# Second-stage rows interleaved by thirds over the partitions, the opening's writes in halves on SyncE, and some evictions behind the first unit's passes

## The chip, the core and the metric

The kernel runs on one core of a Trainium2 chip. Five engines work beside each other, each through its own queue in program order: TensorE (PE; its weight loads are shown as PEld), VectorE (DVE), ScalarE (ACT), GpSimd (POOL) and SyncE (SP). SyncE, ScalarE and GpSimd also issue DMA transfers. The metric is the device time of one execution in microseconds (us).

## What is computed

```python
def _attn_ref(x):                       # x: 8 x 3008 x 256, float32
    X = np.fft.fft(x, axis=1)
    X = np.fft.fft(X, axis=2)
    return X.real.astype(np.float32)

def _moe_ref(x, w_gate, w_val, w_out):  # 24064 x 256; 256 x 1536 twice; 1536 x 256
    g = x @ w_gate
    gelu = 0.5 * g * (1.0 + erf(g * inv_sqrt2))
    val = x @ w_val
    return (gelu * val @ w_out).astype(np.float32)
```

The second function takes the first one's result as 24064 tokens of 256.

## The kernel before

**Splitting.** The 3008 = 64 x 47 points of a batch's sequence are transformed in two stages. The transform over the 256 channels is folded into the weights: `x` is folded into even and odd channel sums (`fold_x`), and the gate and value weights are multiplied by cosine and sine tables once (`gen_w`), giving `WE`, `WOP` and `WOM`. Since the result is real, one half of the sequence gives the other by mirrored rows, called plus and minus.

**First stage.** `load_x` brings a batch in three parts of eight row blocks into `xins` (three buffers of 1 MB). `fold_x` writes `xf`. `a_step(b, k)` makes two products of 128 x 128 with 128 x 256 into one PSUM bank and copies them to `S1`; twelve such steps make the 24 blocks of 128 rows. For batch 0 the banks go round four names; for the others all use `ps_d`, which has one buffer, so each step waits for the copy of the step before it.

**Turning.** The second stage needs other rows side by side. `z_write` stores blocks of `S1` to a scratch `z` in device memory; `z_read` reads it back into `Ap`, 96 partitions of 32 groups x 256. Partition 4 j + r holds rows 32 r to 32 r + 31 of block j. In the opening, block thirds are written from ScalarE's queue and read into 32 neighbouring partitions each. In the other batches there are two writes of 12 blocks and two reads, each of all 96 partitions but of 16 groups: the first read brings groups 0 to 15, the second groups 16 to 31.

**Second stage.** `b_steps(b, eo, q)` makes eight groups' products of 96 x 128 with a table `TP`, `TQ`, `T0P` or `T0Q` (47 columns), for even (`eo` 0) or odd (`eo` 1) channels, and `evac` copies them to `Y`. Each copies the first 24 columns, then the rest. `q` goes over four sets of eight groups. `TW` and `n_step` make one special row for the values' odd part (`NQ`), which goes through device memory (`n_first` for batch 0).

**Tables.** `phase_g`, `phase_c` and `phase_t` make arguments, `reduce_phase` brings them into range, `sin_g`, `sin_c` and `sin_t` take the sine on ScalarE. `cols_t` makes the columns that number the 96 partitions; with `phase_c` it runs on GpSimd in the opening.

**Units.** After the opening a loop runs over 288 units `u`: batch `b`, three column chunks and 12 blocks of 128 of the 1536 inner width; `i` counts the 36 units of a batch. A unit makes layer 1 for its block: `val_even`, `gate_minus` of the unit before, `gate_plus`, `val_odd` of the unit before, with VectorE's and GpSimd's products behind, and eight products of the layer 2 of an earlier chunk (`l2_steps`). Between the passes of a unit stand the next batch's second-stage steps (`fills`): `plan` gives the unit in which each begins. For batches after the first the odd set `q` = 0 begins at i = 18 and q = 2 at i = 23; in the first batch q = 0 begins at i = 21. At the end of unit i stand `fold_x` of a later batch, `a_step` for the next batch (k = i, in batch 0 k = i - 3), a `z_write` after k = 5 and k = 11, and the two `z_read` at k = 12 and 13. At the beginning of units (0, 14, 19) a part of the batch after the next is loaded, in batch 0 at (8, 12, 17). Batches 6 and 7 load nothing. `extra` puts the remaining weight products into units of batch 0.

**Order.** Every engine keeps the program's order (`_InOrder`). All transfers but the opening's three writes and the load of `w_out` go through SyncE's queue: x, weights, z, the special row and 360 stores of results.

**Warming.** `warm` issues products on `ps_d` that nobody reads.

Of the kernel before, what the change touches and what calls it, by code (L numbers as in the profile page):

```python
# [37 lines left out]
def kernel(  # L38
# [73 lines left out]
    col_q = const_pool.tile([128, 1], FP32)  # L112
# [42 lines left out]
    def ps_d():  # L155
        return psum.tile([128, 512], FP32, tag="d", bufs=1, name="ps_d")
# [40 lines left out]
    iota(_sub(rowk, [[1, 33]], 0), [[1, 33]], 0, 0)  # L197
    iota(_sub(rowk, [[1, 31]], 33), [[1, 31]], 1, 0)
    pool.tensor_scalar(rowk, rowk, 1.0 / 64.0, None, op0=ALU.mult)
    pool.memset(NQ[:, :512], 0.0)  # L200
    iota(_sub(rowc, [[1, 128]], 0), [[1, 128]], 0, 0)
    iota(_sub(rowc, [[1, 128]], 128), [[1, 128]], 0, 0)
    pool.memset(_sub(rowc, [[1, 1]], 128), 128.0)
    for k in range(2):
        iota(_sub(rowt, [[1, 2 * N2]], k * 2 * N2), [[1, 2 * N2]], 0, 0)
        iota(_sub(rowt, [[1, MID]], 4 * N2 + k * NJ), [[1, MID]], 0, 0)
        iota(_sub(rowt, [[1, MID - 1]], 4 * N2 + k * NJ + MID), [[1, MID - 1]], 1, 0)
    pool.memset(_sub(rowt, [[NJ, 2]], 4 * N2 + NJ - 1), 0.0)

    wst = []  # L210

# [66 lines left out]
    def cols_t():  # L278
        R = 2 * NJ
        cp = lambda t: _sub(t, [[1, 1]], 0, 0, R)  # L280
        p, ge, jj, f4 = cp(col_p), cp(col_bot), cp(col_j), cp(col_q)
        for t, a, c in ((jj, 0.5, -0.25), (f4, 0.25, -0.375)):
            pool.tensor_scalar(t, p, a, c, op0=ALU.mult, op1=ALU.add)
            pool.tensor_scalar(t, t, MAGIC, None, op0=ALU.add)
            pool.tensor_scalar(t, t, MAGIC, None, op0=ALU.subtract)
        pool.tensor_scalar(ge, jj, -2.0, p, op0=ALU.mult, op1=ALU.add)
        pool.tensor_scalar(cp(col_top), ge, -1.0, 1.0, op0=ALU.mult, op1=ALU.add)
        pool.tensor_scalar(jj, jj, float(HJ), None, op0=ALU.mult)
        pool.tensor_scalar(jj, f4, -float(N2), jj, op0=ALU.mult, op1=ALU.add)
        pool.tensor_scalar(jj, jj, 1.0 / N2, None, op0=ALU.mult)  # L290
        wide = lambda n: _sub(col_bot, [[0, n]], 0, 0, R)
        for o, n, b0, b1 in [(0, 2 * N2, 0.25, 0.25), (2 * N2, 2 * N2, 0.0, 0.25),
                             (4 * N2, NJ, 0.25, 0.0), (4 * N2 + NJ, NJ, 0.0, 0.0)]:
            pool.tensor_scalar(
                _sub(quat, [[1, n]], o, 0, R), wide(n), b1, b0, op0=ALU.mult, op1=ALU.add)

    def phase_t():
        R = 2 * NJ
        W = 4 * N2 + 2 * NJ
# [20 lines left out]
    redc = []  # L320

    def phase_c(t):
        pool.tensor_scalar(col_c[t], col_p, 128.0 * t, 1.0 / C, op0=ALU.add, op1=ALU.mult)
        both = red2_tile()
        redc.append(both)
        for o, n, b0 in ((0, 129, 0.25), (129, 127, 0.5)):
            pool.tensor_scalar(
                both[:, o : o + n], rowc[:, o : o + n], col_c[t], b0, op0=ALU.mult, op1=ALU.add)

    def reduce_c():  # L330
        for both in redc:
# [30 lines left out]
                    WOM[:, i, fs], WOP[:, i, fs], col_m, None, op0=ALU.mult)  # L362

    def gen_wn():
        ps = ps_d()
        for fc in range(NFC):
            for t in range(NCH):
                pe.matmul(
                    ps[:, fc : fc + 1], wb[(fc // 4 * 512, 1)][:, t, fc % 4 * 128 : fc % 4 * 128 + 128],
                    CW[:, t, 1, 0:1], start=(t == 0), stop=(t == NCH - 1))  # L370
        vec.tensor_copy(WNb[:, :], ps[:, :NFC])
        vec.tensor_copy(WN[:, :], WNb[:, :])
# [50 lines left out]
    def a_step(b, k):  # L423

        xf = xf_bufs[b % 2]
        if "S1" not in st[b]:
            st[b]["S1"] = S1_tile()
        S1 = st[b]["S1"]
        ps = (ps_g, ps_v, ps_o, ps_v)[k % 4]() if b == 0 else ps_d()
        for i in range(2):  # L430
            jj = 2 * k + i
            st[b]["mm"] = (pe.matmul(
                ps[:, i * C : (i + 1) * C], G[:, jj, :], _sub(xf, [[1, C]], jj * C),
                start=True, stop=True))
        dst = _sub(S1, [[1, 2 * C]], 2 * k * C)
        if k % 2 == 0 and (b == 0 and k >= 8 or b == 1 and k < 8):
            return (vec.tensor_copy(dst, ps))
        return (act.activation(dst, ps, AF.Copy))
# [6 lines left out]
            z[0:1, 0, :], ap=[[C, 128], [128 * C, nj], [1, C]], offset=z[j0, 0:1, :].offset)  # L445
        eng.dma_start(out=dst, in_=_sub(S1, [[C, nj], [1, C]], j0 * C))

    def z_read(b, g0, ng, j0=0, nj=HJ):
        if "Ap" not in st[b]:
            st[b]["Ap"] = Ap_tile()  # L450
        z, Ap = st[b]["z"], st[b]["Ap"]
        src = ap_replace(
            z[0:1, 0, :], ap=[[NG * C, 4 * nj], [1, ng * C]], offset=z[j0, g0 : g0 + 1, :].offset)
        sync.dma_start(
            out=_sub(Ap, [[1, ng * C]], g0 * C, 4 * j0, 4 * nj), in_=src)

    def b_steps(b, eo, q):

# [25 lines left out]
                        ps[r, o : o + N2], w, t[:, s : s + N2], start=True, stop=True))  # L484
            return run

        def evac():
            ps = box["ps"]
            if Ys[b] is None:
                Ys[b] = Y_tile()  # L490
            Y = Ys[b]
            g0 = 8 * q

            def copy(o, i):
                if b or q % 2:
                    (act.activation(o, i, AF.Copy))
                else:
                    (vec.tensor_copy(o, i))

            copy(  # L500
                _sub(Y, [[32, MID], [1, 8]], eo * YW + g0),
                _sub(ps, [[1, MID], [N2, 8]], 0))
            n2 = N2 - MID
            f = 1 if q == 0 else 0
            copy(
                _sub(Y, [[32, n2], [1, 8 - f]], eo * YW + 32 * MID + g0 + f - 1),
                _sub(ps, [[1, n2], [N2, 8 - f]], MID + f * N2))
            if q == 0:
                copy(
                    _sub(Y, [[32, n2]], eo * YW + 32 * MID + 31), ps[:, MID:N2])  # L510
                copy(
                    _sub(Y, [[1, 1]], eo * YW + NCOL - 1), ps[:, 8 * N2 : 8 * N2 + 1])

        steps = [mm(gi, False) for gi in range(8)]
        if eo == 1 and b == 0:
            steps += [mm(gi, True) for gi in range(8)]
        return steps, evac


    units = []  # L520
# [138 lines left out]
        return steps  # L659


    def warm(n, w):
        ps = ps_d()
        k = w.ap[0][1]
        for _ in range(n):
            pe.matmul(ps, w, _sub(NQ, [[1, 512]], 0, 0, k), start=True, stop=True)

    for t in range(NCH):
        phase_c(t)
    cols_t()  # L670
    still = _sub(NQ, [[1, 128]], 0)
    for i in (1, 0):
        load_w(0, i)
    phase_g(0)
# [5 lines left out]
    for i in range(3):  # L680
        if i:
            fold_x(0, i, vec)
        for k in range(4 * i, 4 * i + 4):
            a_step(0, k)
        warm((5, 2, 4)[i], still)
        z_write(0, 8 * i, 8, act)
        if i == 0:
            sin_g(2)
        z_read(0, 0, NG, 8 * i, 8)
    for i in (1, 0):  # L690
        load_w(512, i)
    load_x(1, 0)
# [1 line left out]
    for i in (1, 0):  # L694
        load_w(1024, i)
    load_x(1, 2)
    reduce_c()
    sin_c()
    pt = phase_t()
    cast_w(0)  # L700
    for i in (1, 0):
        gen_w(0, i, (ps_g, ps_v))
    warm(6, still)
    warm(6, _sub(st[0]["Ap"], [[1, 128]], 0, 0, 64))
    sin_t(*pt)
    act.activation(col_f[:, :], col_p[:, :], AF.Gelu)
    for eo in range(2):
        for q in range(4):
            steps, evac = b_steps(0, eo, q)
            for s in steps:  # L710
                s()
            evac()
    n_first(0)
    cast_w(512)
    load_wo()
    extra = {2: lambda: gen_w(512, 1, (ps_o, ps_o)), 3: lambda: gen_w(512, 0, (ps_o, ps_o)),
# [15 lines left out]
    for u in range(NU + 2):  # L732
# [2 lines left out]
        tail = None  # L735
        if u < NU:
            open_unit(u)
            loads = (0, 14, 19) if b else (8, 12, 17)
            if i in loads and b + 2 < B:
                load_x(b + 2, loads.index(i))  # L740
            if b + 1 < B:
                for what in plan[min(b, 1)].get(i, ()):
                    if what == "n":
                        tail = lambda b=b: n_step(b + 1)
                        continue
                    eo, q, lo, hi = what
# [13 lines left out]
                if l2q:  # L760
                    l2q.pop(0)()

        if u < NU:
            val_even(u)
            fill()
        if 0 < u <= NU:
            gate_minus(u - 1)
            fill()
        if u < NU:
            gate_plus(u, fill)  # L770
            if banks[u]["kd"] == 0:
                plus(banks[u])
# [13 lines left out]
        if u < NU:  # L786
# [57 lines left out]
```

## Time and profile before

Three runs took 658.94, 660.66 and 660.88 us. The profiled execution:

| | |
|---|---|
| its own time | 660.34 us |
| span from first to last instruction | 658.6 us |
| PE busy | 632.5 us, 96% of the span |
| PEld busy | 415.5 us, 63% |
| DVE busy | 529.8 us, 80% |
| ACT busy | 459.3 us, 70% |
| POOL busy | 477.1 us, 72% |
| moved by DMA | 82.69 MB, mean 126 GB/s |
| mean granted TensorE clock | 0.992 |

A line of the page by slices has 40 digits, each the busy share of a slice of 16.5 us in tenths; PEclk is the granted clock in tenths. The chain of waits goes back from the last instruction to whatever released each one. In lists by time, a row has its start, its length, engine, source line, operation, target and source tiles and how many were merged; since a helper issues nearly everything, the source line is L25 for most rows, and rows are told apart by their tiles. SPq is the queue in which SyncE issues transfers: the length there is the issuing, not the transfer. A row of waits names who waited, for whom, the microseconds, how often and the longest.

The opening in a few rows: the x loads are issued from 0.74 us on, the first fold begins at 6.26, the first product at 8.88, the third write of batch 0's z is issued at 16.97, weight products run from 20.20 to 24.0, the second stage from 29.01 to 32.88, and the units begin there.

### The profile page before, as it was taken

What the parts mean: (1) busy time and instruction counts of PE and PEld (TensorE: products, weight loads), DVE (VectorE), ACT (ScalarE), POOL (GpSimd) and SP (SyncE); (2) the same over time, 40 slices, a digit from 0 to 9 for tenths busy, and PEclk for the clock granted to TensorE, in tenths of its full rate; (3) what the DMA queues carried; (4) which work ended last, traced back from release to release, by engine and by line L of the source; (5) the groups of instructions that cost most, each with busy time, mean ns of one, the idle gap of its engine ahead of it and who ended that gap; (6) DMA issues with size and microseconds to landing.
All of it is one profiled execution on the core that took longest, in us unless ns stands there. A gap on an engine that the chain in (4) does not pass through costs nothing.

```text
span 658.6 us, 14004 instructions
## 1 busy us (share of the span) xinstructions
PE 632.5 (96%) x4593; PEld 415.5 (63%) x4647; DVE 529.8 (80%) x860; ACT 459.3 (70%) x976; POOL 477.1 (72%) x777
## 2 busy tenths in 40 slices
PE   4698999999999999999999999999999999999997
PEld 2344666666666666666666666676666666666666
DVE  8567877797868988698777988689887987789981
ACT  8477677767678676776677676786767766666662
POOL 8294899977897598886897778975986544745450
PEclk9889999999999999999999999999999999999999
DMA  8993822456233832348224652328321452211123
GB/s 297 270 328 112 237 75 56 136 153 199 71 109 83 248 112 63 112 125 263 65 49 142 161 193 69 110 82 250 114 59 52 126 140 60 49 44 37 47 49 77
DMA packets 66089, 82.69 MB, mean 126 GB/s; under 512 B 8031, under 2 KB 58943, under 8 KB 62528
## 3 DMA queue, kind: packets, MB, share of 16 engines
q1 hardware_dynamic: 61344, 79.44, 41.7%
q0 software_dynamic: 1552, 0.79, 0.9%
q10 hardware_dynamic: 3120, 1.57, 0.8%
q8 instruction: 36, 0.59, 0.4%
q14 instruction: 37, 0.30, 0.2%
HBM read 45.13 MB, written 37.44 MB: 125 GB/s over the span
## 4 chain that ended last, share of the span: by engine, by line
PE 89%; DVE 6%; DMA 2%; ACT 1%; issue 1%; ACTq 0%; DVEq 0%
PE ps_o L25 38%; PE ps_g L25 26%; PE ps_v L25 20%; PE ps_d L25 6%; DVE h L25 2%; DVE xf L25 1%; DMA z<-S 1%; DMA Ap<-z 1%; ACT gl L25 1%; DVE ev L25 1%; DVE red L25 1%; DVE S L25 0%; DVE dv L25 0%; DVE WOM L25 0%; DVE sa L25 0%
## 5 line engine op out<-in xcount | busy, mean ns | idle before, releaser
L25 ACT ACTIVATE gl<-ps_g 128x512 bf16<-128x512 f32 (+1 forms) x576 | 309.4, 587 | 147.2 <-PE ps_g L25 104.7
L25 POOL TENSOR_TENSOR h<-gl,dv 128x512 bf16<-128x512 bf16 (+1 forms) x216 | 246.8, 1143 | 147.1 <-DVE dv L25 101.7
L25 DVE TENSOR_TENSOR h<-gl,ps_v 128x512 bf16<-128x512 bf16 (+2 forms) x360 | 237.4, 676 | 102.8 <-ACT gl L25 84.9
L25 PE MATMUL ps_o<-Wo_sb,h 128*128 128x256 bf16 (+2 forms) x2304 | 296.7, 273 | 0.0
L25 PEld LDWEIGHTS <-h 128*128 128x128 bf16 (+2 forms) x2304 | 227.0, 100 | 65.2 <-issue 1.8
L25 DVE SCALAR_TENSOR_TENSOR ev<-nq,WN,ps_v 128x512 f32<-128x512 bf16 (+1 forms) x216 | 157.5, 729 | 2.8 <-PE ps_v L25 2.8
L25 POOL TENSOR_TENSOR xf<-xin 128x127 bf16<-128x127 f32 (+1 forms) x312 | 141.7, 475 | 7.7 <-DMA xin<-in_x_dram 7.7
L25 DVE SCALAR_TENSOR_TENSOR dv<-ev,ps_v 128x512 f32<-128x512 f32 (+1 forms) x216 | 144.2, 667 | 0.0
L25 PE MATMUL ps_v<-Y,WE 128*128 128x512 bf16 (+1 forms) x287 | 108.4, 378 | 0.2 <-issue 0.2
L25 PE MATMUL ps_g<-Y,WOM 128*128 128x512 bf16 (+1 forms) x288 | 107.7, 374 | 0.1
L25 PE MATMUL ps_g<-Y,WOP 128*128 128x512 bf16 (+1 forms) x281 | 105.3, 375 | 2.0
L25 PE MATMUL ps_v<-Y,WOP 128*128 128x512 bf16 (+1 forms) x281 | 105.7, 376 | 0.4
L25 PE MATMUL ps_g<-Y,WE 128*128 128x512 bf16 (+1 forms) x250 | 93.7, 375 | 0.0
L25 PEld LDWEIGHTS <-WOP 128*128 128x128 bf16 x576 | 56.0, 97 | 47.1 <-issue 1.1
L25 ACT ACTIVATE osb<-ps_o 128x512 f32<-128x512 f32 (+2 forms) x112 | 58.3, 535 | 33.0 <-PE ps_o L25 29.8
L25 PEld LDWEIGHTS <-WE 128*128 128x128 bf16 x576 | 56.2, 98 | 25.3 <-issue 1.9
L25 PEld LDWEIGHTS <-Ap 96*128 96x128 bf16 (+3 forms) x574 | 43.6, 98 | 39.1 <-issue 11.2
L25 ACT ACTIVATE S<-ps_d 128x512 bf16<-128x512 f32 x80 | 48.3, 603 | 3.5 <-PE ps_d L25 3.5
L25 PEld LDWEIGHTS <-WOM 128*128 128x128 bf16 x360 | 35.0, 97 | 16.6 <-issue 0.8
L25 PEld LDWEIGHTS <-G 128*128 128x128 bf16 x192 | 19.0, 100 | 33.3 <-ACT G L25 6.3
L25 ACT ACTIVATE Y<-ps_d 128x192 bf16<-128x192 f32 (+4 forms) x142 | 37.3, 349 | 0.6 <-PE ps_d L25 0.6
L25 PE MATMUL ps_d<-xf,G 128*128 128x256 bf16 x168 | 32.0, 272 | 2.0 <-DVE S L25 1.5
(107 smaller groups left out, 284.7 us busy)
## 6 DMA issues: line engine op xcount, KB each, us to landing
out_dram<-osb SPq DMA_DIRECT2D x360, 64.0 KB
xin<-in_x_dram SPq DMA_DIRECT2D x16, 1024.0 KB
z<-S SPq DMA_DIRECT2D x14, 768.0 KB
Ap<-z SPq DMA_DIRECT2D x14, 768.0 KB
xin<-in_x_dram SPq DMA_DIRECT2D x8, 896.0 KB
ngr<-nrow SPq DMA_DIRECT2D x7, 388.0 KB
wst<-in_moe_w_val_dram SPq DMA_DIRECT2D x3, 512.0 KB
wst<-in_moe_w_gate_dram SPq DMA_DIRECT2D x3, 512.0 KB
```

The lines of the kernel that those rows point to most:

```text
L25: return lambda *a, **k: self._tc.keep_in_program_order(call(*a, **k))
```

## The change

- **Rows.** The turning of all batches goes by thirds: third t has blocks 8 t to 8 t + 7, all 32 groups, and goes to partitions t, t + 3, t + 6 and so on. The columns and tables are made for that numbering (`col_q` is three columns now). In the loop the three reads stand at k = 12, 13 and 14 (two at 12 and 13 before); the writes stay at k = 5 and 11 with 12 blocks each. In batch 0 the third x load moves from unit 17 to 18; in the others the loads stay at (0, 14, 19).
- **Opening's transfers.** The writes go through SyncE; the second and third in halves of four blocks. The first read is issued between the halves of the second write, the other two at the end.
- **Table work.** `cols_t` is first on GpSimd, and the constant parts of `quat` are clears. `phase_c` moves from GpSimd to ScalarE (with constant bias columns) and behind the first stage. `phase_t` comes before it, `sin_t` before the weight products. The clear of NQ is gone.
- **Warming** multiplies `G` by `G`, 5, 2 and 10 products in the opening's steps and 6 ahead of the second stage, instead of 5, 2, 4, 6 and 6.
- **Banks.** `gen_wn` uses `ps_o`; `a_step` of batch 1 uses `ps_o` in steps 1, 3, 5 and 7.
- **First unit.** The odd sets' copies are split: the first 24 columns behind their products, the rest behind the four passes of unit 0, which are written out in a new order.

```diff
-    pool.memset(NQ[:, :512], 0.0)
-    iota(_sub(rowc, [[1, 128]], 0), [[1, 128]], 0, 0)
-    iota(_sub(rowc, [[1, 128]], 128), [[1, 128]], 0, 0)
...
+    def cols_t():
+        R = 2 * NJ
+        cp = lambda t: _sub(t, [[1, 1]], 0, 0, R)
+        p, ge, jj, f3, f6, f12 = (cp(t) for t in (col_p, col_bot, col_j, *col_q))
+        for t, d in ((f3, 3), (f6, 6), (f12, 12)):
+            pool.tensor_scalar(t, p, (1.0 - d) / 2, 1.0 / d, op0=ALU.add, op1=ALU.mult)
+            pool.tensor_scalar(t, t, MAGIC, None, op0=ALU.add)
+            pool.tensor_scalar(t, t, MAGIC, None, op0=ALU.subtract)
+        pool.tensor_scalar(ge, f6, -2.0, f3, op0=ALU.mult, op1=ALU.add)
+        pool.tensor_scalar(cp(col_top), ge, -1.0, 1.0, op0=ALU.mult, op1=ALU.add)
+        pool.tensor_scalar(f6, f3, -1.0, f6, op0=ALU.mult, op1=ALU.add)
+        pool.tensor_scalar(f6, f6, 3.0, p, op0=ALU.mult, op1=ALU.add)
+        pool.tensor_scalar(jj, f12, -float(N2), None, op0=ALU.mult)
+        pool.tensor_scalar(jj, f6, 8.0, jj, op0=ALU.mult, op1=ALU.add)
+        pool.tensor_scalar(jj, jj, 1.0 / N2, None, op0=ALU.mult)
+
+    cols_t()
+    TO = 4 * N2
+    iota(_sub(rowt, [[2 * N2, 2], [1, 2 * N2]], 0), [[0, 2], [1, 2 * N2]], 0, 0)
+    iota(_sub(rowt, [[NJ, 2], [1, MID]], TO), [[0, 2], [1, MID]], 0, 0)
+    iota(_sub(rowt, [[NJ, 2], [1, MID - 1]], TO + MID), [[0, 2], [1, MID - 1]], 1, 0)
+    pool.memset(_sub(rowt, [[NJ, 2]], TO + NJ - 1), 0.0)
+    for o, b0 in ((0, 0.25), (2 * N2, 0.0)):
+        pool.tensor_scalar(
+            _sub(quat, [[1, 2 * N2]], o, 0, 2 * NJ), _sub(col_bot, [[0, 2 * N2]], 0, 0, 2 * NJ),
+            0.25, b0, op0=ALU.mult, op1=ALU.add)
+    pool.memset(_sub(quat, [[1, NJ]], TO), 0.25)
+    pool.memset(_sub(quat, [[1, NJ]], TO + NJ), 0.0)
+    iota(_sub(rowc, [[128, 2], [1, 128]], 0), [[0, 2], [1, 128]], 0, 0)
     pool.memset(_sub(rowc, [[1, 1]], 128), 128.0)
-    for k in range(2):
-        iota(_sub(rowt, [[1, 2 * N2]], k * 2 * N2), [[1, 2 * N2]], 0, 0)
-        iota(_sub(rowt, [[1, MID]], 4 * N2 + k * NJ), [[1, MID]], 0, 0)
-        iota(_sub(rowt, [[1, MID - 1]], 4 * N2 + k * NJ + MID), [[1, MID - 1]], 1, 0)
-    pool.memset(_sub(rowt, [[NJ, 2]], 4 * N2 + NJ - 1), 0.0)
+    for i in range(2):
+        pool.memset(bias_c[i], 0.25 * (i + 1))
...
-        pool.tensor_scalar(col_c[t], col_p, 128.0 * t, 1.0 / C, op0=ALU.add, op1=ALU.mult)
+        vec.tensor_scalar(col_c[t], col_p, 128.0 * t, 1.0 / C, op0=ALU.add, op1=ALU.mult)
         both = red2_tile()
         redc.append(both)
-        for o, n, b0 in ((0, 129, 0.25), (129, 127, 0.5)):
-            pool.tensor_scalar(
-                both[:, o : o + n], rowc[:, o : o + n], col_c[t], b0, op0=ALU.mult, op1=ALU.add)
+        for q, (o, n) in enumerate(((0, 129), (129, 127))):
+            act.activation(both[:, o : o + n], rowc[:, o : o + n], AF.Identity,
+                           scale=col_c[t][:, :], bias=bias_c[q][:, :])
...
     def gen_wn():
-        ps = ps_d()
+        ps = ps_o()
...
-        ps = (ps_g, ps_v, ps_o, ps_v)[k % 4]() if b == 0 else ps_d()
+        if b == 0:
+            ps = (ps_g, ps_v, ps_o, ps_v)[k % 4]()
+        else:
+            ps = ps_o() if b == 1 and k % 2 and k < 8 else ps_d()
...
-    def z_read(b, g0, ng, j0=0, nj=HJ):
+    def z_read(b, third):
         if "Ap" not in st[b]:
             st[b]["Ap"] = Ap_tile()
         z, Ap = st[b]["z"], st[b]["Ap"]
         src = ap_replace(
-            z[0:1, 0, :], ap=[[NG * C, 4 * nj], [1, ng * C]], offset=z[j0, g0 : g0 + 1, :].offset)
-        sync.dma_start(
-            out=_sub(Ap, [[1, ng * C]], g0 * C, 4 * j0, 4 * nj), in_=src)
+            z[0:1, 0, :], ap=[[NG * C, 32], [1, NG * C]], offset=z[8 * third, 0:1, :].offset)
+        p_step = Ap[:, :, :].ap[0][0]
+        dst = ap_replace(
+            Ap[:, :, :], ap=[[3 * p_step, 32], [1, NG * C]],
+            offset=Ap[:, :, :].offset + third * p_step)
+        sync.dma_start(out=dst, in_=src)
...
-        def evac():
+        def copy(o, i):
+            if b or q % 2:
+                (act.activation(o, i, AF.Copy))
+            else:
+                (vec.tensor_copy(o, i))
+
+        def evac_top():
             ps = box["ps"]
             if Ys[b] is None:
                 Ys[b] = Y_tile()
-            Y = Ys[b]
-            g0 = 8 * q
-
-            def copy(o, i):
-                if b or q % 2:
-                    (act.activation(o, i, AF.Copy))
-                else:
-                    (vec.tensor_copy(o, i))
-
             copy(
-                _sub(Y, [[32, MID], [1, 8]], eo * YW + g0),
+                _sub(Ys[b], [[32, MID], [1, 8]], eo * YW + 8 * q),
                 _sub(ps, [[1, MID], [N2, 8]], 0))
+
+        def evac_rest():
+            ps, Y, g0 = box["ps"], Ys[b], 8 * q
             n2 = N2 - MID
             f = 1 if q == 0 else 0
             copy(
...
         steps = [mm(gi, False) for gi in range(8)]
         if eo == 1 and b == 0:
             steps += [mm(gi, True) for gi in range(8)]
-        return steps, evac
+        def evac():
+            evac_top()
+            evac_rest()
+
+        return steps, evac, evac_top, evac_rest
...
-    def warm(n, w):
+    def warm(n):
         ps = ps_d()
-        k = w.ap[0][1]
         for _ in range(n):
-            pe.matmul(ps, w, _sub(NQ, [[1, 512]], 0, 0, k), start=True, stop=True)
-
-    for t in range(NCH):
-        phase_c(t)
-    cols_t()
-    still = _sub(NQ, [[1, 128]], 0)
+            pe.matmul(ps, G[:, 0, :], _sub(G, [[1, 512]], 0), start=True, stop=True)
+
     for i in (1, 0):
         load_w(0, i)
     phase_g(0)
...
             fold_x(0, i, vec)
         for k in range(4 * i, 4 * i + 4):
             a_step(0, k)
-        warm((5, 2, 4)[i], still)
-        z_write(0, 8 * i, 8, act)
+            if i == 0 and k == 3:
+                z_write(0, 0, 8)
+            elif i and k % 2:
+                z_write(0, 2 * k - 2, 4)
+                if k == 5:
+                    z_read(0, 0)
+        warm((5, 2, 10)[i])
         if i == 0:
             sin_g(2)
-        z_read(0, 0, NG, 8 * i, 8)
+    for i in (1, 2):
+        z_read(0, i)
     for i in (1, 0):
         load_w(512, i)
     load_x(1, 0)
...
     for i in (1, 0):
         load_w(1024, i)
     load_x(1, 2)
+    pt = phase_t()
+    for t in range(NCH):
+        phase_c(t)
     reduce_c()
     sin_c()
-    pt = phase_t()
+    sin_t(*pt)
     cast_w(0)
     for i in (1, 0):
         gen_w(0, i, (ps_g, ps_v))
-    warm(6, still)
-    warm(6, _sub(st[0]["Ap"], [[1, 128]], 0, 0, 64))
-    sin_t(*pt)
     act.activation(col_f[:, :], col_p[:, :], AF.Gelu)
+    warm(6)
+    later_evacs = []
     for eo in range(2):
         for q in range(4):
-            steps, evac = b_steps(0, eo, q)
+            steps, evac, evac_top, evac_rest = b_steps(0, eo, q)
             for s in steps:
                 s()
-            evac()
-    n_first(0)
+            if eo:
+                evac_top()
+                later_evacs.append(evac_rest)
+            else:
+                evac()
...
-            loads = (0, 14, 19) if b else (8, 12, 17)
+            loads = (0, 14, 19) if b else (8, 12, 18)
...
+        if u == 0:
+            r = banks[0]
+            r["pv"], r["pg"] = ps_v(), ps_g()
+            layer1(r, r["pv"], WE, 1, 0, r["n"], True)
+            layer1(r, r["pg"], WE, 0, 0, r["n"], True)
+            layer1(r, r["pg"], WOP, 0, 1, r["n"], False)
+            layer1(r, r["pv"], WOP, 1, 1, r["n"], False)
+            for e in later_evacs:
+                e()
+            n_first(0)
+            r["glp"] = gl_tile()
+            act.activation(r["glp"][:, :], r["pg"], AF.Gelu)
+            plus(r)
+        elif u < NU:
             val_even(u)
             fill()
         if 0 < u <= NU:
             gate_minus(u - 1)
             fill()
-        if u < NU:
+        if 0 < u < NU:
...
-                elif k in (12, 13):
-                    z_read(b + 1, 16 * (k - 12), 16)
+                elif k in (12, 13, 14):
+                    z_read(b + 1, k - 12)
```

More of the change, by code (lines that the diff above doesn't have):

```diff
@@ L111 @@
     col_j = const_pool.tile([128, 1], FP32)
-    col_q = const_pool.tile([128, 1], FP32)
+    col_q = [const_pool.tile([128, 1], FP32, name=f"col_q{i}") for i in range(3)]
+    bias_c = [const_pool.tile([128, 1], FP32, name=f"bias_c{i}") for i in range(2)]
     col_m = const_pool.tile([128, 1], FP32)
@@ L276, in sin_g @@
                 _sub(reds[i], [[64, 8], [1, 64]], 0), AF.Sin, scale=col_h[h][:, :])
[L278 to L293, printed above, removed]
-            pool.tensor_scalar(
-                _sub(quat, [[1, n]], o, 0, R), wide(n), b1, b0, op0=ALU.mult, op1=ALU.add)
     def phase_t():
@@ L322, in phase_c @@
     def phase_c(t):
-        pool.tensor_scalar(col_c[t], col_p, 128.0 * t, 1.0 / C, op0=ALU.add, op1=ALU.mult)
+        vec.tensor_scalar(col_c[t], col_p, 128.0 * t, 1.0 / C, op0=ALU.add, op1=ALU.mult)
         both = red2_tile()
         redc.append(both)
-        for o, n, b0 in ((0, 129, 0.25), (129, 127, 0.5)):
-            pool.tensor_scalar(
-                both[:, o : o + n], rowc[:, o : o + n], col_c[t], b0, op0=ALU.mult, op1=ALU.add)
+        for q, (o, n) in enumerate(((0, 129), (129, 127))):
+            act.activation(both[:, o : o + n], rowc[:, o : o + n], AF.Identity,
+                           scale=col_c[t][:, :], bias=bias_c[q][:, :])
     def reduce_c():
@@ L768 @@
             fill()
-        if u < NU:
+        if 0 < u < NU:
             gate_plus(u, fill)
```

## The prediction

> **What bounds the kernel now.** First the page: engines by slice, then the chain that ended last.
>
> ```profile
> PE   4698999999999999999999999999999999999997
> ...
> PEclk9889999999999999999999999999999999999999
> ...
> PE 89%; DVE 6%; DMA 2%; ACT 1%; issue 1%; ACTq 0%; DVEq 0%
> ```
>
> TensorE is full from the third slice on, and 89% of the chain is its own work. What it does not wait for costs nothing; a wait put into it costs its whole length. The long chain's pieces show the one place where transfers set the end, the opening:
>
> ```profile
> 16.97 6.14 DMA z<-S
> 23.13 5.84 DMA Ap<-z
> ```
>
> The first batch's third write goes out at 16.97, the last read of it at 23.13, and the second stage starts at 29.0. Next the clock and the stretch after it, in stretches of 3.41 us (columns: stretch and its length, busy us and instructions of PE, PEld, DVE, ACT and POOL, granted clock, DMA share, GB/s):
>
> ```profile
> 13.78:17.20 3.42, 2.81 (x18) 1.55 (x16) 2.92 (x6) 2.71 (x6) 2.93 (x10) 1.00 0.56 135
> 17.20:20.61 3.41, 0.39 (x1) 0.10 (x1) 3.38 (x5) 0.63 (x2) 2.22 (x4) 1.00 0.98 253
> 20.61:24.02 3.41, 3.15 (x8) 1.16 (x9) 1.34 (x4) 1.99 (x4) 0.00 (x0) 0.50 1.06 285
> ```
>
> After two stretches with PE busy 3.20 of 6.83 us (47%), one runs at half clock. Then the waits of the one-buffer tile ps_d between 41 and 62 us:
>
> ```profile
>   DVE S L25: 2.3, 3
>   DVE WNb L25: 0.5, 1
> ```
>
> PE stood 2.8 us there. Last, one steady batch: SyncE's queue, TensorE at the first use of Ap, who held SyncE, and the bytes moved:
>
> ```profile
> 142.34 0.79 SPq L25 DMA_DIRECT2D Ap<-z  x2
> 143.23 0.57 SPq L25 DMA_DIRECT2D xin<-in_x_dram  x1
> ...
> 149.73 0.20 PE L25 MATMUL ps_d<-T0Q,Ap 96*128 96x47 bf16 x2
> ...
> SPq L607 <- DMA xin<-in_x_dram: 2.2, 1, 2.2
> ...
> 153.84 0.32 SPq L607 DMA_DIRECT2D out_dram<-osb  x1
> ...
> 143.30:149.70 6.40, 6.35 (x43) 4.13 (x43) 5.04 (x9) 3.75 (x7) 3.68 (x4) 1.00 0.99 244
> 149.70:153.80 4.10, 4.05 (x35) 2.77 (x35) 4.10 (x8) 3.11 (x9) 1.17 (x1) 1.00 0.97 349
> ```
>
> Both reads and the x load leave SyncE within a microsecond. By 149.70 the queue has moved 244 GB/s x 6.40 us = 1.56 MB, which is the two reads (2 x 0.786 MB) and none of x: it serves in order. The x load lands when it lets SyncE's store go at 153.84. PE's first use at 149.73 finds its data because it needs only groups 0 to 15, the first read.
>
> **The change, part by part.** The sum is made against the profiled execution: 660.34 us, span 658.6, so 1.7 us lie around the span; the median of the runs is 660.66.
>
> *Reads by thirds in the steady batches.* Each third fills every third partition with all 32 groups, and the second stage contracts over 96 partitions: its first matmul now needs all three reads. In the built program that load of weights waits for three transfers where it waited for one. The third read is issued at the end of unit 14; the x load of batches 1 to 5 still goes out at the beginning of unit 14. So SyncE's order is read, read, x load, read, and the last read takes the place that x had. The bytes are the same (3 x 0.524 against 2 x 0.786 MB), so its landing is bounded by that of x before. Read like 153.84, x landed at 153.84, 231.05, 307.47, 383.84 and 460.54; the first uses stood at 149.73, 226.48, 303.22, 379.98 and 456.73: 4.1, 4.6, 4.3, 3.9 and 3.8 us earlier, mean 4.1. The first third needs only the first write, so it need not stand the 0.5 us for which SyncE waits on the second write: 3.6 us of wait per batch, 5 x 3.6 = 18.0 us. Behind the waiting weights stand all of TensorE's later passes, for them ScalarE, VectorE and GpSimd; steady PE idle is 2.8 us in all, so nothing makes it up. Ends: if 2.62 MB went at the 426 GB/s that the x loads show at 4 to 8 us, they would take 6.2 us from 143.3, and be in place at 149.5: no wait. If the thirds are as slow as the opening's last one (23.13 to 28.97, 5.84 us with its latency), the wait stays near 4.6. I take 3.5, 17.5 us, because the nearest row has the same queue, bytes, neighbours and moment.
>
> [...]
>
> Batches 0 and 6 have no load between (batch 0's third load moves from unit 17 to 18 for that; batch 6 loads nothing), but they too need all three reads. The second read of before lets SyncE go at 151.34 in the batch above, 1.6 after the first use; less 0.5 for the earlier start and about as much for the stores among it, 0.5 each: +1.0. Ends 0 and 2.2.
>
> *The clock after such a wait.* Row: 47% busy over 6.83 us was followed by 3.41 us at half clock, which loses 1.7 us of work. A wait of 3.5 us leaves 49% if one such pair of stretches holds it, 75% if two share it. I take every second of the five: 5 x 0.5 x 1.7 = 4.3 us; ends 0 and 5 x 3.4 = 17 (6.83 us at half clock, as from 30.85 to 37.67, each time).
>
> [...]
>
> *Opening: writes on SyncE, in halves.* First half of block two leaves at about 14.45 (its second ACT eviction ends at 14.43) instead of 15.44 with the whole; the transfers, idle at 15 to 16, start earlier, and a half less stands behind. The three reads then queue back to back. Against: the first read stands behind a write that ACT's queue had beside it. I put the second stage's data at 26.5 instead of 29.0: some 1.5 us from the earlier writes and 1 us from reads without a gap. It cannot start before the weights and tables: the cosine weights come off VectorE later (ACT builds their phase, 4 activations of about 0.3, after VectorE's table phase), I put PE's weight products at 21.3 instead of 20.20, eight of them at half clock 3.4 us, then six warm-ups: 26 to 27. So 2.3 us gained; ends 0 and 3.4.
>
> *GpSimd's casts.* They come when GpSimd ends its small operations, 16 or so against 17 before, one for each VectorE fold pass (1.13 us) while folds run: about 16, after the folds. VectorE's 256-wide two-input pass took 2.75 us beside these casts and 0.42 alone, so 2.3 us is the price if they fall on the third fold instead; I take nothing, since the fold ends at 14.84. The removed NQ clear (0.52), the merged iotas and the phase moves are inside waits for x.
>
> *Odd steps and the WN product on ps_o.* Of the 2.8 us, step 3 gets some back: it follows weight products that fill both ps_o buffers, whose eviction takes 0.6. 2.2 gained; ends 0 and 2.8.
>
> *Evictions behind unit 0's passes.* Unit 0 needs columns 0 to 511, all in the top parts. PE's gap there is 0.22 us at half clock: taken as 0.5 with whatever clock window is gained; ends 0 and 2.4 (half of 30.85 to 37.67 less the 2 us of second stage).
>
> Sum: -2.3 - 2.2 - 0.5 + 17.5 + 1.0 + 4.3 = +17.8, so 660.3 + 17.8 = 678 us. Against the median it is the same to 0.3 us.
>
> **Rivals.**
> 1. *The last read is on time; the opening's gain shows.* One mechanism: thirds over scattered partitions move near 426 GB/s. For it: the x loads do; the DMA engines are 0.99 busy at 244 GB/s, so something other than the number of packets slows the reads. Against: no row shows a 96-partition target filled faster; the packets of one queue and their neighbours stay. It decides from 3.6 us less per batch: 660.3 - 5.0 = 655.
> 2. *A short wait.* Reads a third quicker: 1.1 us late in five batches, no clock loss, batches 0 and 6 nothing: 660.3 + 5.5 - 5.0 = 661.
> 3. *The wait, and no gain in the opening.* Casts fall on the third fold, writes land 2.3 later, the clock drops after each wait: 660.3 + 17.5 + 1.0 + 8.5 - 2.2 = 685. Against: the count of small operations above.
> That the change does not do what it says is excluded for the order: it stands in the built program.
>
> **How the numbers follow.** Forecast 0.72; rival 1 0.13; rival 2 0.07; rival 3 0.08. The forecast's own range, with rival 3, is 667 to 688: 2.7 to 4.2 us per wait, 0 to 8.5 of clock, 1 to 8 of opening. To leave out no more than 2 in 10 I take 662 to 687. Below 0.3% (2 us) a change can't be told from none. Rival 1 is faster, 0.13; rival 2 lies around no change and gives it 0.06 and 0.01 to slower; slower 0.81.
>
> **What would show it.** PE waiting in five places, about 80 us apart (76.75 between first uses before, and the wait), for DMA Ap<-z, 3 to 4 us each, the x load moved before the landing, and the clock at 0.50 after some of them; second stage at 26 to 27; no PE idle on ps_d at 41 to 62. Wrong: no row of PE waiting for Ap after 60 us, or a last third that lands within 7 us of the first's issue.

## The result, and the profile after

Four runs of the changed kernel took 683.51, 689.18, 689.41 and 692.78 us, median 689.29; the kernel before beside them has a median of 660.77. The ratio is 1.0427, with a 95% interval of 1.0352 to 1.0501: slower by 28.5 us. The forecast of 678 had the sign and the mechanism, not the size, and 689.3 lies above its range of 662 to 687. The profiled execution is the slowest of the four, 692.78 us, with a span of 691.0 against 658.6 before (+32.4); a second profile, of an execution of 687.76 us and so nearer the median, follows below.

The page of the changed kernel: engines and granted clock in 40 slices, then the chain that ended last, by engine.

```profile
PE   4688999989999899997999979999899999999997
...
PEclk9799999999999999998999999999999999999999
...
PE 81%; DMA 10%; DVE 4%; issue 1%; ACT 1%; POOL 1%; SPq 0%; ACTq 0%; DVEq 0%; POOLq 0%
```

Before, TensorE's line was nothing but nines from the fifth slice to the last but one. Now there is a dent about every five slices, which is one batch, and transfers have 10% of the chain instead of 2%. The waits of TensorE say for what (columns: total us, how often, the longest):

```profile
PE ps_d L25 <- DMA Ap<-z: 12.3, 5, 3.7
PE ps_d L25 <- DMA out_dram<-osb: 8.9, 2, 4.8
PE ps_v L25 <- DMA Ap<-z: 2.8, 1, 2.8
```

Seven waits at `ps_d`: one in each of batches 0 to 6. The last row is the opening's. Two of the seven are put down to a store of results, and this must be read with care. The weights there wait for the third read's semaphore, and so does a store on the same semaphore; in the batch of 321 us TensorE's wait ahead of that load ends at 320.92, and the store leaves in the same moment:

```profile
310.50 0.60 SPq L25 DMA_DIRECT2D Ap<-z  x1
...
320.90 0.32 SPq L623 DMA_DIRECT2D out_dram<-osb  x1
```

So both are the third read's landing. One steady batch, the one that the prediction showed, in SyncE's queue and then in TensorE's (the time in brackets is the idle time before the row):

```profile
144.61 1.19 SPq L25 DMA_DIRECT2D Ap<-z  x2
145.89 0.59 SPq L25 DMA_DIRECT2D xin<-in_x_dram  x1
146.54 0.59 SPq L25 DMA_DIRECT2D Ap<-z  x1
```

```profile
152.25 0.38 PE L25 MATMUL ps_v<-Y,WE 128*128 128x512 bf16 x1
156.08 0.20 PE L25 MATMUL ps_d<-T0Q,Ap 96*128 96x47 bf16 x2 [3.46 <-DMA Ap<-z]
```

Read, read, x load, read; and TensorE stands until 11.47 us after the first of them. The clock around it (the columns of the prediction's stretches):

```profile
149.00:152.42 3.42, 3.42 (x25) 2.23 (x23) 2.07 (x4) 1.99 (x4) 2.29 (x2) 1.00 0.87 290
152.42:155.83 3.41, 0.21 (x1) 0.00 (x0) 2.23 (x4) 0.60 (x1) 1.70 (x3) 1.00 1.00 306
155.83:159.24 3.41, 3.16 (x16) 1.71 (x17) 0.69 (x1) 1.19 (x2) 1.38 (x5) 0.50 0.65 174
```

One stretch with 0.21 us of work, and the next at half clock. Last the opening, in the chain's long pieces:

```profile
16.97 5.04 DMA z<-S
22.07 7.14 DMA Ap<-z
```

The last write is 1.1 us shorter than before and the last read goes out 1.06 earlier, but takes 1.3 longer: the second stage starts at 29.35, not earlier than the 29.01 before.

The delay against before, taken at the same unit's Gelu in both traces, gives the account. "Again" is a second profile of the changed kernel, from the last experiments; a batch's increment is the change of the delay over it, its wait is TensorE's idle time before the first use of `Ap` plus about 0.15 us for the modelled end of the matmul ahead (such a product is shown with 0.38 us, and the next one starts 0.21 to 0.22 us after it), and the rest of the increment is put down to the clock. (The clock's own rows fit that: behind the five waits they have 18.9 us at half clock in this profile and 19.4 in the second, which is 9.4 and 9.7 us of lost work.)

| us | forecast | profile after | again |
|---|---|---|---|
| opening, up to unit 12 | -5.0 | +1.3 | -2.7 |
| five waits, batches 1 to 5 | +17.5 | +20.0 | +19.6 |
| half clock behind them | +4.3 | +9.0 | +9.1 |
| batches 0 and 6 | +1.0 | +2.2 | +1.5 |
| sum | +17.8 | +32.5 | +27.5 |

### The profile page after: what moved, and what is told of

It reads as the page before. It is cut to its first block, busy times and chain, and to the rows that moved or that the text cites. A ratio compares the mean times of both kernels' runs of the same rounds, so it can differ in the third digit from the quotient of the medians.

```text
span 691.0 us, 14083 instructions
## 1 busy us (share of the span) xinstructions
PE 645.4 (93%) x4647; PEld 418.9 (61%) x4647; DVE 535.3 (77%) x862; ACT 461.9 (67%) x980; POOL 475.8 (69%) x773
## 4 chain that ended last, share of the span: by engine, by line
PE 81%; DMA 10%; DVE 4%; issue 1%; ACT 1%; POOL 1%; SPq 0%; ACTq 0%; DVEq 0%; POOLq 0%
PE ps_o L25 34%; PE ps_g L25 24%; PE ps_v L25 18%; DMA Ap<-z 7%; PE ps_d L25 5%; DMA out_dram<-osb 1%; DVE h L25 1%; DVE WOM L25 1%; DVE xf L25 1%; DMA xin<-in_x_dram 1%; ACT gl L25 1%; DMA z<-S 1%; DVE dv L25 1%; POOL h L25 1%; DVE S L25 0%
## 5 line engine op out<-in xcount | busy, mean ns | idle before, releaser
L25 PE MATMUL ps_o<-Wo_sb,h 128*128 128x256 bf16 (+2 forms) x2304 | 300.7, 275 | 0.0
L25 PE MATMUL ps_g<-Y,WOP 128*128 128x512 bf16 (+1 forms) x288 | 109.2, 379 | 0.0
L25 PE MATMUL ps_g<-Y,WE 128*128 128x512 bf16 (+1 forms) x288 | 109.1, 379 | 0.0
L25 PE MATMUL ps_v<-Y,WOP 128*128 128x512 bf16 (+1 forms) x288 | 108.3, 376 | 0.0
L25 PEld LDWEIGHTS <-Ap 96*128 96x128 bf16 (+2 forms) x568 | 44.1, 101 | 63.1 <-issue 28.2
L25 ACT ACTIVATE S<-ps_d 128x512 bf16<-128x512 f32 x76 | 45.9, 604 | 0.0
L25 PEld LDWEIGHTS <-G 128*128 128x128 bf16 x215 | 21.8, 102 | 38.8 <-issue 11.0
L25 PE MATMUL ps_v<-Y,WOM 128*128 128x512 bf16 (+1 forms) x72 | 28.3, 392 | 3.4 <-DVE h L25 3.4
```

The source lines that it names most:

```text
L25: return lambda *a, **k: self._tc.keep_in_program_order(call(*a, **k))
```

## The experiments

The kernel before ran beside each of them, with medians of 660.3 to 661.0 us. A number to follow in the traces is the time from the issue of the first of the three reads to the first product that needs them: 12.1 us in the changed kernel, mean of batches 1 to 5 (11.47, 11.48, 13.02, 11.98, 12.46).

**The place in the queue.** e1 lets the x load out a unit later, so that all three reads stand ahead of it.

```diff
-            loads = (0, 14, 19) if b else (8, 12, 18)
+            loads = (0, 15, 19) if b else (8, 12, 18)
```

> Only change to the changed kernel: in batches 1 to 5 the second x load is issued at unit 15 instead of 14, so the third read stands ahead of it in SyncE's queue. Theory (place in the queue): the third read lands some 2.5 us (1 MB at 426 GB/s) earlier, the five waits shrink from 3.2 to 4.8 us to about 1 us, like those of batches 0 and 6 now, and the clock mostly holds: 689 - 5 x (2.7 + 1.3) = 669 us. Rival (rows scattered over the partitions are slow to fill, whatever stands ahead): waits of about 3 us stay, over 680 us.

664.31 us (662.99 to 666.45), ratio 1.0073 [1.0052, 1.0095]: the theory, and 5 us better than its 669. From first issue to first use it is 9.3 us, and TensorE's waits are 0.62 to 2.14 us. SyncE's queue in the same batch:

```profile
137.72 1.82 SPq L25 DMA_DIRECT2D Ap<-z  x3
140.09 1.77 SPq L623 DMA_DIRECT2D out_dram<-osb  x4
141.96 0.60 SPq L25 DMA_DIRECT2D xin<-in_x_dram  x1
```

Over batches 1 to 5 the delay grows by 6.3 us instead of 29.0, so 22.7 us are the x load's place ahead of the third read, with the clock that goes with it: no half clock falls behind any of these waits. What is left is 8.3 us between unit 12 and the end: even unhindered, three thirds come after the moment at which the first half sufficed (first issue to first use 9.3 us, where the kernel before has 7.39 in the batch shown, 142.34 to 149.73).

**The thirds undone, the rest of the change kept.** e2 reads by groups again, into the new numbering.

```diff
-                elif k in (12, 13, 14):
-                    z_read(b + 1, k - 12)
+                elif k in (12, 13):
+                    z_half(b + 1, 16 * (k - 12))
```

> The changed kernel with the steady batches' reads by group halves again (two reads of 96 partitions x 16 groups at k = 12 and 13), into the scattered rows' numbering; the opening and all else as changed. Theory (the first product needs all three thirds): no wait for Ap after the opening, so what is left is the opening's own effect, +1.3 us by unit 12 in the changed kernel's profile: 662 us. Rival (the opening gained what I forecast and something steady took it): 655 to 657 us.

654.70 us (654.25 to 655.99), ratio 0.992 [0.9905, 0.9935]. The products no longer wait for `Ap` behind the opening, and the lead of 5.6 us that stands at unit 12 is kept to the end; it was the rival that named this lead. So all of the steady loss is the thirds', and this version is faster than both kernels, than the one before by 0.8%.

**The thirds alone.** e3 is the kernel before with nothing but the steady reads by thirds, each into 32 neighbouring partitions (and batch 0's load moved with them).

```diff
-                elif k in (12, 13):
-                    z_read(b + 1, 16 * (k - 12), 16)
+                elif k in (12, 13, 14):
+                    z_read(b + 1, 0, NG, 8 * (k - 12), 8)
```

> The kernel before with only the steady batches' reads changed: three thirds into 32 neighbouring partitions each at k = 12, 13, 14, third x load of batch 0 at unit 18; rows, tables and opening as before. Theory (place in the queue): the last bytes land where x landed before, so five waits of 3.5 to 4.5 us and half clock after them, 660.8 + 5 x 5.6 + 2 = 690 us. Rival (scattered rows are what is slow): waits at most half as long, below 677 us.

704.53 us (703.99 to 705.79), ratio 1.0674 [1.0658, 1.069]. The waits are 4.39 to 5.90 us in batches 1 to 5, and half clock follows six of the seven. It was slower than either theory said: from first issue to first use it is 13.2 us here, and the next run tells why.

**The spread over the partitions.** e4 is the changed kernel with the row numbering of before, so that a third fills 32 neighbouring partitions instead of every third one.

```diff
-            Ap[:, :, :], ap=[[3 * p_step, 32], [1, NG * C]],
-            offset=Ap[:, :, :].offset + third * p_step)
+            Ap[:, :, :], ap=[[p_step, 32], [1, NG * C]],
+            offset=Ap[:, :, :].offset + 32 * third * p_step)
```

> The changed kernel with its rows numbered as before: every third goes into 32 neighbouring partitions, in the opening and after it; the order of everything as changed. If scattered rows make a read no slower and no faster: 689 us again, and the opening's last two reads take 7 us from the first issue to the landing of the second plus 1.5, as now. If scattered rows slow the reads (two of 16 parts of the opening's last read came 2.8 us after the others): the second stage begins about 2 us earlier than 29.35 and the waits are shorter, below 684 us. If they speed the reads: over 692 us.

702.17 us (699.28 to 705.71), ratio 1.0638 [1.0595, 1.0682]: 13 us more than the changed kernel. First issue to first use is 13.7 us instead of 12.1. The row that answers to 156.08 above:

```profile
153.87 0.20 PE L25 MATMUL ps_d<-T0Q,Ap 96*128 96x47 bf16 x2 [5.92 <-DMA out_dram<-osb]
```

So the interleaving itself is a gain, some 1.6 us a batch in the landing and more with the clock; it is spent on reads that are all needed at once.

**Wait and clock apart.** e8 keeps the changed kernel's queue and fills the wait with products that nobody reads.

```diff
+            if 1 <= b <= 5 and i == 18:
+                warm(14)
             val_even(u)
```

> The changed kernel with 14 products more (128 columns by 512, about 3.0 us at full clock, into a ps_d bank that nobody reads) ahead of the unit whose products wait for the third read, in batches 1 to 5. The reads are as late as before, so the second stage's rows arrive at the same time; TensorE is busy in most of the 3.4 to 4.9 us. Theory (each of the five waits costs its own length and then 1.7 us of half clock behind it): the gaps shrink to about 1 us, the half clock behind them goes, and the time falls by about 5 x 1.8 = 9 us to 679 to 682 us. Rival (the clock falls whether TensorE is busy or not, or the loss of 9 us isn't the clock's): 687 us or more.

679.30 us (678.52 to 680.68), ratio 1.0279 [1.0231, 1.0327]. The reads land as late as before (first issue to first use 12.5 us, and what is left of the waits is 0.45 to 2.45 us), yet it is 9.2 us less than the repeated run of the changed kernel. Its stretches around the same wait:

```profile
141.00:144.41 3.41, 3.41 (x26) 2.28 (x24) 2.06 (x4) 2.11 (x4) 2.33 (x2) 1.00 0.92 293
144.41:147.83 3.42, 3.36 (x17) 1.33 (x14) 1.72 (x4) 0.60 (x1) 1.57 (x3) 1.00 1.01 306
147.83:151.24 3.41, 3.02 (x26) 1.92 (x27) 2.15 (x3) 1.49 (x3) 1.50 (x5) 1.00 0.67 167
```

The clock stays at 1.00 in all five places. In the profiles some 7 of the 9.2 us are the steady batches' (increments of 22.0 over batches 1 to 5 against 28.7), the rest is the opening. The first uses come 0.5 us a batch later here than in that run (12.5 against 12.0 us), so at equal landings the five drops of the clock would be worth some 9 us, an estimate from these numbers.

**The banks alone.** e6 is the kernel before with the bank edits and nothing else.

```diff
-        ps = ps_d()
+        ps = ps_o()
...
+            ps = ps_o() if b == 1 and k % 2 and k < 8 else ps_d()
```

> The kernel before with nothing changed but the banks: products of the second batch's first stage with odd k below 8, and the products for the Nyquist columns, go to ps_o instead of ps_d. Theory (the two waits for a ps_d bank in the first batch, 2.2 us as forecast, go, and nothing else): 660.4 - 2.2, between 657.7 and 659 us. Rival (the products then wait for ps_o, or the time lies elsewhere in the first batch): 660 us or more.

657.81 us (655.17 to 658.56), ratio 0.995 [0.9932, 0.9968], 2.6 us less. In its profile 2.0 us of it come between units 6 and 12, where the two rows of idle time at `ps_d` that the prediction showed are gone.

**The opening's parts.** Each of these differs from e2 in one part: e5 has the row numbering of before; e7 makes `WOM` on ScalarE; e9 has the opening's writes whole and on ScalarE's queue, with a read behind each; e10 has the first unit and its evictions as before. Their cores:

```diff
# e7
-                vec.tensor_scalar(
-                    WOM[:, i, fs], WOP[:, i, fs], col_m, None, op0=ALU.mult)
+                act.activation(WOM[:, i, fs], WOP[:, i, fs], AF.Copy, scale=col_m[:, :])
# e9
+        z_write(0, 8 * i, 8, act)
# e10
-            if eo:
-                evac_top()
-                later_evacs.append(evac_rest)
-            else:
-                evac()
+            evac()
+    n_first(0)
```

> The changed kernel with the row numbering of the kernel before (rows of one third on 32 neighbouring partitions in the opening) and the steady reads by halves behind the x load's second and third part, as before. It differs from e2_halves_scattered (654.7 us) in the spread of the opening's three thirds alone. Theory (the spread is worth 13 us over the seven batches whose thirds are waited for, so below 2 us for the opening's single last third; e4's opening ended 4.6 us early against e2's 5.6): 655 to 656.5 us, delay against before at unit 12 between -4.0 and -5.2 us. Rival (the spread carries the opening's gain): above 657.5 us, delay at unit 12 above -3 us. No wait of the products for Ap behind the opening in either.

> e2_halves_scattered with the sign-turned weights WOM made by ScalarE (copy with a scale by row) instead of VectorE. In the changed kernel's profile two of VectorE's WOM passes took 3.25 and 4.03 us where others took 0.35, beside GpSimd's folds and casts, and the products waited 1.2 and 1.4 us for them. Theory (VectorE is held by GpSimd; ScalarE isn't): the ScalarE passes take under 1 us each, no product waits over 0.5 us for WOM, and the time is 653.5 to 655 us, since e2's own WOM passes were 0.8 us at most. Rival (ScalarE is needed for evictions there and becomes the wait): 656 us or more.

> e2_halves_scattered (654.7 us) with the opening's z writes as before: one of eight rows for each third, on ScalarE's queue, and each third's read behind it. Theory (halving the writes and moving them to SyncE is worth what the second stage's start shows, 28.64 against 29.01 us before, so about 0.4 us, not the 2.3 of the forecast): 654.7 to 656 us, second stage's products from 28.8 to 29.6 us. Rival (the transfers are the opening's gain after all): 656.5 us or more, second stage from 30 us on.

> e2_halves_scattered (654.7 us) with the first unit as before: the evictions of the odd rows' lower part and the Nyquist products ahead of the unit's first passes, and its gate and value passes in the old order. The forecast put the evictions behind the passes at 0.5 us. Theory (it is more, since of e2's 5.6 us the second stage's start has 0.4 and the banks 2.0, which leaves 3.2 for evictions and the opening's clock): 656 to 657.7 us, and delay at unit 6 against before between -0.5 and -2.5 us, at unit 12 2 us less than at unit 6. Rival (the evictions are worth 0.5 or nothing and the rest is the clock's luck): 654.2 to 655.5 us.

In this order: 656.98 us (ratio 0.9937 [0.9912, 0.9963]), 656.17 (0.9939 [0.9915, 0.9962]), 656.04 (0.9938 [0.991, 0.9967]) and 656.80 (0.9939 [0.9919, 0.996]). By these numbers e7 has its rival's time, e10 its theory's, and e5 and e9 lie between the two. But single runs of the four go from 654.4 to 662.1, so e2 was run again:

> e2_halves_scattered once more (654.7 us in four runs). e5, e7, e9 and e10 each differ from it in one part of the opening and took 656.0 to 657.0 us, their single runs 654.4 to 662.1. Theory (the opening varies from run to run by a half clock that does or does not fall behind the second stage, about 2 us, and none of these parts is worth more than about 1 us): a median of 654.7 to 656.5 us with single runs up to 658 or so. Rival (each of those parts is worth its 1.3 to 2.3 us): 654.2 to 655.2 us, with hardly a run above 656.

656.28 us (653.86 to 658.00), ratio 0.9919 [0.989, 0.9947]: the medians of all four lie within what e2's own runs take, 653.86 to 658.00 us, so none of the four parts is shown to be worth anything. The two profiles of this one kernel show how its runs come to differ. The same three stretches, first of e2, then of e11:

```profile
27.44:30.85 3.41, 2.43 (x75) 2.06 (x74) 1.54 (x7) 1.35 (x7) 1.04 (x1) 1.00 1.07 382
30.85:34.27 3.42, 3.33 (x41) 1.83 (x40) 1.75 (x6) 2.09 (x6) 3.00 (x4) 1.00 1.02 417
34.27:37.68 3.41, 3.39 (x16) 1.38 (x15) 2.44 (x4) 2.88 (x7) 3.41 (x7) 1.00 1.03 355
```

```profile
27.44:30.85 3.41, 1.88 (x54) 1.43 (x53) 1.06 (x6) 1.18 (x6) 0.15 (x1) 0.99 1.03 353
30.85:34.27 3.42, 3.42 (x53) 2.42 (x52) 1.52 (x7) 1.38 (x5) 3.13 (x3) 0.50 1.02 419
34.27:37.68 3.41, 3.19 (x9) 1.21 (x9) 0.69 (x1) 1.53 (x4) 3.20 (x8) 0.51 1.02 390
```

In e2 the clock held behind the second stage; in e11 two stretches ran at half clock, and unit 12 came 3.3 us later. The ten profiles with the changed opening's writes line up by this. Where the clock held there (e1, e2, e4, e8), the lead at unit 12 is 4.6 to 5.8 us; with one stretch at half clock (e5) it is 4.1; with two (e7, e10, e11 and both of the changed kernel) it is 3.3 at most. What decides over it stays open. It is not the start of the second stage, 28.64 us in e2 and 29.36 in e11: in e4 it starts at 29.29 and the clock holds, in e10 at 28.37 and it does not. Nor is it how busy TensorE was in the stretch ahead, in e4 and then in e10:

```profile
25.51:28.92 3.41, 1.50 (x6) 0.49 (x5) 0.35 (x1) 2.25 (x4) 0.00 (x0) 1.00 0.83 195
28.92:32.33 3.41, 3.04 (x95) 2.76 (x95) 1.81 (x9) 1.42 (x5) 1.61 (x2) 1.00 1.04 410
```

```profile
26.12:29.53 3.41, 1.60 (x45) 1.15 (x44) 0.74 (x5) 0.86 (x5) 0.00 (x0) 1.00 1.01 323
29.53:32.94 3.41, 3.41 (x61) 2.54 (x59) 1.96 (x10) 1.56 (x7) 3.04 (x3) 0.50 1.03 425
```

**The changed kernel again.**

> The changed kernel once more, for a second profile of its opening. Its first profile lost 1.3 us by unit 12, where e2_halves_scattered, which has the same opening, gained 5.6, and VectorE held two of the WOM passes for 3.25 and 4.03 us there. Theory (the opening differs from run to run, and the steady part's loss does not): median within 683 to 693 us, delay at unit 12 anywhere from -6 to +2 us, and between unit 18 and the last unit +29 to +33 us with a half clock behind each of the five waits. Rival (the opening's loss belongs to the changed kernel): delay at unit 12 again above 0.

688.54 us (686.87 to 689.39), ratio 1.0435 [1.0393, 1.0476]. The opening gained 2.7 us this time, and the steady part lost 30.1 (31.2 in the first profile), as the theory had it: see the table above.

## Why the prediction was right in kind and short in size

Against the second profile, the one near the median, the sum is 9.7 us short: 4.8 of it is the clock, 2.3 the opening, 2.1 the five waits and 0.5 batches 0 and 6. In the first profile, the slowest execution, it is 14.7, and there the opening is the largest part with 6.3.

**The wait: right, and short by a seventh.** It was to come from the third read's taking x's place. e1 shows that place; the first of the five waits is 3.6 us with the modelled end, as worked out, but the later ones reach 4.9, so the mean is 4.0 and not 3.5: 20.0 for 17.5. Batches 0 and 6, taken at 0.5 each, together lost 2.2 and 1.5 in the two profiles: e1 shows the same, for three thirds without x among them still take 9.3 us to the first use. One reading was weaker than the forecast had it: that the 1.56 MB moved by 149.70 are just the two reads can't be seen from bytes alone, since by its own row the second read lets SyncE go only at 151.34. The order of landing that it took from this, reads before x, is what e1 confirms.

**The clock: the step that failed most.** The sum took "every second of the five", 4.3 us; all five dropped, in both profiles, and cost 9.0. e8 shows that this is the clock's own price and not the wait's: landings no earlier, TensorE busy, no drop, about 7 us back. The reasoning over pairs of stretches (49% busy in one pair, 75% when two share the wait) was wrong, because such a pair is not the condition: one stretch that is nearly empty, 0.21 us of 3.41, was enough, with a full one ahead of it. In all ten waits of the two profiles the stretch ahead of the half clock had at most 1.07 us of work; with the one before it that is up to 55% of the pair.

What the traces show of the length of a wait: of those on `Ap` behind the opening all 20 of 3.10 to 6.46 us (both profiles of the changed kernel, e3, e4) were followed by half clock, some of it before the wait was over, and of 22 of 0.45 to 2.50 us (these, e1 and e8) one was, of 1.96 us in e3. The length alone does not cover the opening: in the kernel before the clock fell at 30.85 although TensorE's longest idle time in the seven microseconds ahead was 1.31 us.

**The opening: the transfers' term failed.** They were to bring 2.3 us by starting the second stage at 26 to 27. In ten profiles with the changed opening's writes it started at 28.17 to 29.36, mean 28.8, against 29.0 before, so 0.2 us; with the writes as before (e9) at 28.39. The earlier issue of the last read, 22.07 to 22.60 us against 23.13, is mostly given back as a longer read, 5.92 to 7.14 us for 5.84. Both parts of the term fell with it, the 1.5 us from earlier writes and the 1 us from reads without a gap. The banks were right (2.2 forecast, 2.6 measured in e6). The evictions at 0.5 are not told from nothing by e10. So where the forecast's -5.0 was reached or passed (e1, e2, e8), it was by luck: the clock held behind the second stage. That gain the forecast had named as the upper end of the evictions' term (2.4 us) and then priced within its 0.5.

**GpSimd's casts at nothing: right where it was looked for.** They ran from 15.59 to 17.62, behind the folds. But a like price came up later, in the first units (last section).

**The rivals.** The first, thirds near 426 GB/s, fell; so did the short wait. The third, 685 us, came nearest by number: its clock behind each wait is what happened, while its reason for no gain in the opening, casts on the third fold, is not.

The spread over the partitions, for which the sum has no term, shows in e4: 13 us are lost without it, and from first issue to first use e4 and the changed kernel are 1.6 us apart (13.7 and 12.1). It did not bring the reads in time: the third read still was first used 9.5 to 10.5 us after its issue, behind x.

## What to carry to other kernels

When a read is cut in pieces another way, ask of each consumer which pieces its first instruction needs: halves by column let work start on the first one, thirds by partition need all three, and then the last piece's place in the queue sets the time. Price a wait on TensorE with the clock behind it: here every wait of 3.10 us or more cost its length and, in the mean, 1.8 us again in the changed kernel and 2.2 to 2.4 in e4 and e3, whose waits are longer. And undo a change part by part: the opening and the banks of this one are worth some 5 us (4.8 and 5.6 in the two runs of e2's kernel), once the steady reads are left as they were.

## What was unexpected in the hardware

VectorE's pass for `WOM` takes 0.34 to 0.36 us at its shortest, even beside GpSimd's folds (48.59 us in the second profile). In the changed kernel's first profile:

```profile
40.72 3.25 DVE L25 TENSOR_SCALAR WOM<-WOP,col_m 128x512 bf16<-128x512 bf16 x1
...
45.08 0.45 DVE L25 TENSOR_SCALAR WOM<-WOP,col_m 128x512 bf16<-128x512 bf16 x1
...
50.53 4.03 DVE L25 TENSOR_SCALAR WOM<-WOP,col_m 128x512 bf16<-128x512 bf16 x1
```

```profile
50.03 1.40 POOL L25 TENSOR_TENSOR xf<-xin 128x254 bf16<-128x254 f32 x2
51.38 0.19 POOL L25 CAST xf<-xin 128x4 bf16<-128x4 f32 x1
51.52 1.40 POOL L25 TENSOR_TENSOR xf<-xin 128x254 bf16<-128x254 f32 x2
...
54.56 0.62 POOL L25 COPY TW<-TP 96x12 bf16<-96x12 bf16 x2
```

GpSimd's folds of 0.7 us follow each other without a gap from 50.03 to 54.56, and the pass that began at 50.53 ends at 54.56. The pass from 40.72 likewise ends at 43.97, the moment at which GpSimd goes from one fold to the next. TensorE stood 1.2 and 1.4 us behind these two, at 44.61 and 55.22 (its wait is put down to VectorE's product `h`, which stands behind the pass). That is 2.7 of the 4.0 us by which this profile's opening is behind the second one's, where TensorE has no such wait. In other profiles of the same opening the longest pass took 0.78 (e2) to 1.83 us (e11), so it differs from run to run, and that GpSimd holds the pass is argued from the times at which it ends, not shown by a run of its own; on ScalarE (e7) every one took 0.72, without a gain in time that the runs could show.
